# RWKV-7 scan and hard-swish FFN on one core: the decay input w of units 8 to 23 is loaded in 32-token quadrants and turned on VectorE

## The chip, the cores and the metric

The kernel runs on one core of a Trainium2 chip. The metric is device time in microseconds for one execution of the program. The core's engines, as the profile names them: PE (TensorE, matrix products and its weight loads PEld), DVE (VectorE), ACT (ScalarE), POOL (GpSimd) and SP (SyncE, which here issues DMA transfers). Each engine, and SP's queue of transfers too, works through its own instructions in program order.

## The reference

Two blocks follow one another. The first is a recurrence over 768 tokens for each of 4 x 8 heads with a 40 x 40 state; the second a feed-forward block over the 3072 tokens of 320 features.

```python
for t in range(S):                              # r, k, v, w, a, b: (4, 8, 768, 40)
    y[:, :, t] = np.einsum('bhd,bhde->bhe', rt, state)
    Sa = np.einsum('bhde,bhe->bhd', state, at)
    state_decay = state * wt[:, :, None, :] - np.einsum('bhd,bhe->bhde', Sa, bt)
    state = state_decay + np.einsum('bhd,bhe->bhde', vt, kt)
x = attn_out.transpose(0, 2, 1, 3).reshape(B * S, H * D)
h = x @ w_in                                    # (320, 2048)
g = h * np.clip(h + 3.0, 0.0, 6.0) / 6.0
return g @ w_out                                # (2048, 320)
```

What matters here is w: the per-token, per-feature decay. The kernel needs its running products along the tokens.

## The kernel before

**Units.** The recurrence is done in chunks of 64 tokens (`BL`). A unit is one chunk of two batches and all 8 heads; `NU` = 4 units belong to a group and there are `NK` = 24 units, 0 to 23. A unit's input tile has 128 partitions (two batches of 64 tokens) and 8 heads of 64 slots (`SLOT`), of which 40 hold features; the rest is padding, 1.0 for w. Each unit has a part that does not depend on the state (`prepare`, lines 524 to 700) and a part that does (`step`, lines 820 to 1009).

**What the preparation does.** `w_stage` (L527) turns w on TensorE, so that features lie on partitions and tokens along the row: four transposes of 128x128 against an identity (L474, in `turn_pairs`) into a PSUM bank. Two ScalarE copies (L537 and L541) bring it from PSUM into `wm`, the scan's input: 16 rows of 33 per partition, for 4 head pairs, 2 batches and 2 halves of 32 tokens, the first half in reversed token order. Then the next unit's w is fetched, and a VectorE scan (L544) makes the running products. `gam_stage` adds a reciprocal, a second scan (L555) and copies. `a_stage`, `b_stage` and `k_stage` turn a, b and k on TensorE and multiply them with what came out of the scans; `F`, `factor`, `E` and `EV` follow. `factor_stage` multiplies K and B on POOL (L663), then fetches this unit's V (L455) and the next unit's B and K (L458). V is read by the next block's EV products (L690).

**What the step does.** `s_RT` and `s_VT` turn r and v; R, C, U, UT, rS, sn, H and y are products; the result is summed on VectorE (L983, into ys), scaled on POOL (L984, into yg), and `s_move` and `s_move2` put it by eight SBUF-to-SBUF transfers (L998, L1003) into `xt`, the input of the feed-forward block.

**Feed-forward.** `expand` (L1054) makes the hidden products from xt, 96 matrix products to a unit; ScalarE and VectorE apply the activation (L1069, L1070); `contract` (L1095) makes the output, which ScalarE copies (L1113) and SP stores (L1119). It runs as a stream in small pieces between the pieces of the recurrence.

**Order.** The order on every engine is fixed by hand. From group 2 on (units 8 and up) the program goes in blocks, four to a unit's step. In `a_block` a unit in preparation contributes its stages block by block (`AHEAD_STAGES`, or `CLOSE_STAGES` where units follow after three blocks), beside the steps of an earlier unit (`OWN_STAGES`). `together` (L1328) runs the stages of one block: first the TensorE products of all stages, in the order of `PRODUCTS`, as far as five PSUM banks go; then what drains them, in the order of `RESULTS`. `TURNS` are the stages at the head of `PRODUCTS` that take a bank or half a pair each. A stage that is not in `PRODUCTS` is run with the last drain of its block. Transfers are issued by the stages as they come, nearly all on SP's queue. Where an inversion runs (once per group, `invert`), VectorE has many small instructions beside these (L741, L747).

**Loads.** `fetch` (L434) loads one input of one unit: for W, A, B and K one transfer for each of two batches, 64 tokens x 8 heads in rows of 40 floats (160 bytes); for R and V two per batch. W, A, B, K and R of the next unit are fetched when this unit's tile has been read (`following`).

Of the kernel before, what the change touches and what calls it, by code (L numbers as in the profile page):

```python
# [18 lines left out]
BL = 64  # L19
HB = BL // 2  # L20
L = 32
SLOT = 64
# [3 lines left out]
def _ap(ap, extra, dims):  # L26

    return bass.AP(tensor=ap.tensor, offset=ap.offset + extra, ap=[list(ap.ap[0])] + dims)
# [3 lines left out]
def kernel(  # L32
# [42 lines left out]
    nc = tc.nc  # L75
    B, H, T, D = r.shape
# [3 lines left out]
    NU = 2 * NP  # L80
# [38 lines left out]
    def ps_any(shape):  # L119
        tag, bufs = ring[0]  # L120
        ring.rotate(-1)
        at = 0
        if tag == "whole":
            t = pair()
            open_half[0] = None
        elif tag != "pair":
            t = bank(tag, [P, 512], bufs)
        elif open_half[0] is None:
            t = open_half[0] = pair()
        else:  # L130
            t, at = open_half[0], 512
            open_half[0] = None
        views, step = [], 1
        for d in reversed(shape[1:]):
            views.insert(0, [step, d])
            step *= d
        return _ap(t[:], at, views)
# [3 lines left out]
    def ps_pair(*dims):  # L141
# [21 lines left out]
        out=ident[:], in_=ones, pattern=[[1, P]],  # L163
# [4 lines left out]
        out=ones[:, 0:BL], in_=ones[:, 0:BL], pattern=[[1, BL]],  # L168
# [3 lines left out]
        out=ones[BL:P, 0:BL], in_=ones[BL:P, BL:P], pattern=[[1, BL]],  # L172
# [15 lines left out]
    PADS = {"W": 1.0}  # L188
# [18 lines left out]
    SCAN = NB * 2 * (HB + 1)  # L207
# [3 lines left out]
    wms = [const.tile([P, SCAN + 1], F32, name=f"wm{i}") for i in range(2)]  # L211
# [10 lines left out]
    for i in range(3):  # L222
        t = const.tile([P, H, BL], F32, name=f"score{i}")
# [14 lines left out]
    for p in range(NP):  # L238
        t = const.tile([P, 2, NPR, SLOT], F32, name=f"state{p}")
        nc.vector.memset(t[:], 0.0)  # L240
        state.append(t)
        t = const.tile([P, 2, NPR], F32, name=f"last{p}")
# [16 lines left out]
    for i, (x, y) in enumerate([(0, DFF // 2), (0, NJ // 2)]):  # L259
        for n, z in enumerate((x, y)):  # L260
            t = win[:, :, z:z + H * SLOT] if i == 0 else \
                wout[:, z:z + 4, :].rearrange("p j m -> p (j m)")[:, 0:2 * H * SLOT].rearrange(
                    "p (n x) -> p n x", n=2)
            t = t.rearrange("p n (h e) -> p n h e", e=SLOT)
            name = ("WA", "BK")[i][n]
# [3 lines left out]
    for u in range(2):  # L269
        t = win2[:, u * NPR * P:(u + 1) * NPR * P]  # L270
# [160 lines left out]
    names = [(2 * (i // NU) + i % NU // NP, i % NP) for i in range(NK)]  # L431
    data = [{} for _ in range(NK)]

    def fetch(name, i, engine=None):  # L434

        if i is None or i >= NK:
            return
        x, crossed = {"W": (w, 0), "A": (a, 0), "B": (b, 0), "K": (k, 0), "R": (r, 1),
                      "V": (v, 1)}[name]
        if name == "V":  # L440
            t = values[i % AHEAD]
        else:
            t = placed.get((name, i))
            if (name, i) == ("R", 1):
                t = others["K"]
            t = t if t is not None else (others if i < 2 * NU and i % 2 and name != "R" else inputs)[name]
        g, p = names[i]
        engines = engine or nc.sync
        for q in range(2):
            engine = engines[q] if isinstance(engines, tuple) else engines  # L450
            y = x[2 * p + q, :, g * BL:(g + 1) * BL, :]
            rows = slice(q * BL, (q + 1) * BL)
            if crossed:
                for s in range(2):
                    engine.dma_start(out=t[rows, 4 * s:4 * s + 4, 0:D],  # L455
                                     in_=y[s::2].rearrange("h t e -> t h e"))
            else:
                engine.dma_start(out=t[rows, :, 0:D], in_=y.rearrange("h t e -> t h e"))  # L458
        data[i][name + "N"] = t

    def following(i):

        if i < 2:
            return None
        if i < 2 * NU:

            return i + 2 if i % NU < NU - 2 or i % 2 == 0 else None
        return i + 1

    def turn_pairs(x):  # L470

        o = ps_any([P, NPR, P])
        for n in range(NPR):
            nc.tensor.transpose(out=o[:, n, :],  # L474
                                in_=x[:, 2 * n:2 * n + 2, :].rearrange("p s e -> p (s e)"),
                                identity=ident[:])
        return o
# [46 lines left out]
    def prepare(i, F):  # L524
        n, o = i % NU, data[i]
        halves = i >= 2 * NU
        def w_stage():  # L527
            wt = turn_pairs(o["WN"])
            yield PE

            wm = o["wm"] = wms[i % 2]
            wv = wm[:, 0:SCAN].rearrange("p (r m i) -> p r m i", m=2, i=HB + 1)
            x = wt[:].rearrange("p r (q m i) -> p (r q) m i", q=2, m=2)
            if i == 0:
                nc.vector.tensor_copy(wv[:, :, 0, 1:HB + 1], x[:, :, 0, ::-1])
            else:
                nc.scalar.activation(out=wv[:, :, 0, 1:HB + 1], in_=x[:, :, 0, ::-1], func=AF.Copy)  # L537
            if i == 0:
                nc.vector.tensor_copy(wv[:, :, 1, 1:HB + 1], x[:, :, 1, :])
            else:  # L540
                nc.scalar.activation(out=wv[:, :, 1, 1:HB + 1], in_=x[:, :, 1, :], func=AF.Copy)  # L541
            fetch("W", following(i))
            prods = o["prods"] = tmp.tile([P, NB, 2, HB + 1], F32, name="prods", bufs=2)
            nc.vector.tensor_tensor_scan(  # L544
                out=prods[:].rearrange("p r m i -> p (r m i)"), data0=wm[:, 0:SCAN], data1=start[:],
                initial=0.0, op0=ALU.mult, op1=ALU.add,
            )

        def gam_stage():
# [28 lines left out]
            if NU <= i <= 2 * NU:  # L578
                fetch("V", i)
            yield from ()  # L580

        def a_stage():
            x = turn_in(o["AN"], halves)
            yield PE
            nc.vector.memset(_ap(o["wm"][:], 0, [[HB + 1, 2 * NB + 1]]), 0.0)
            at = o["at"] = grp.tile([P, NPR, P], F32, name="at", tag="at")
            for y, z, g in zip(parts_of(at, halves), x, parts_of(o["G"], halves)):
                nc.vector.tensor_tensor(out=y, in0=z, in1=g, op=ALU.mult)
            fetch("A", following(i))
# [93 lines left out]
        def ev_stage():  # L683
# [10 lines left out]
            for x in range(2):  # L694
                nc.scalar.activation(out=EV[half(x)], in_=ev[2][half(x)][:, ::-1] if x else ev[2][half(x)],  # L695
                                     func=AF.Copy)
            o["EV"] = EV

        return {"W": w_stage, "gam": gam_stage, "A": a_stage, "B": b_stage, "F": f_by_32 if i < 2 * NU else f_by_64,
                "factor": factor_stage, "K": k_stage, "E": e_stage, "EV": ev_stage}  # L700

# [524 lines left out]
    n, cleared = 0, []  # L1226
    while not third:
        aside(1)
        if not third:
# [3 lines left out]
            if converted[0] >= 2 and not cleared:  # L1233
                cleared.append(True)
                for z in range(0, P, BL):
                    nc.scalar.activation(out=tinv[z + L:z + BL, :, 0:L], func=AF.Copy, scale=0.0,
                                         in_=_ap(three[z + L:z + BL], 0, [[0, NH], [0, L]]))
# [67 lines left out]
    for _ in range(18):  # L1305
# [10 lines left out]
    CLOSE_STAGES = [["W", "gam"], ["A", "B"], ["F", "K", "factor"], ["E"], ["EV"]]  # L1316


    PRODUCTS = ["W", "S", "K", "RT", "VT", "A", "B", "factor",
                "y", "EV", "R", "C", "U", "UT", "rS", "sn", "H", "E", "F"]  # L1320
    RESULTS = ["RT", "y", "W", "VT", "EV", "R", "S", "C", "A", "B", "move", "move2",
               "U", "UT", "rS", "F", "K", "sn", "H", "E", "factor", "gam"]
    TURNS = PRODUCTS[:3]
    WIDTH = {"R": NPR * D, "U": NPR * D, "sn": NPR * D, "EV": NPR * D}
    BLOCKS = 4
    FIRST_NARROW = PRODUCTS[len(TURNS)]

    def together(stages):  # L1328
# [3 lines left out]
        def finish():  # L1332
            begun.sort(key=lambda x: RESULTS.index(x[0]))
            for _, rest in begun:
                for _ in rest:
                    pass
            begun.clear()
            shared[0] = open_half[0] = None
            ring.clear()
            ring.extend(TURNS_IN)  # L1340

        for name in PRODUCTS:
            if name == FIRST_NARROW and narrow and spread[0] and stages:
                narrow[0]()
            for stage in stages.get(name, []):
                if name in TURNS:
                    need = 2 * (open_half[0] is None) if ring[0][0] == "pair" else 1
# [3 lines left out]
                if banks + need > 5:  # L1351
                    finish()
                    banks, need = 0, 1 if name in TURNS else 2
                banks += need
                rest = stage()
                next(rest)
                begun.append((name, rest))
        begun.extend((name, stage()) for name in stages if name not in PRODUCTS
                     for stage in stages[name])
# [35 lines left out]
    m = 0  # L1395
# [61 lines left out]
```

## Time and profile before

| what | value |
|---|---|
| three runs | 797.92, 798.93, 802.25 us; median 798.93 us |
| span of the profiled execution | 802.0 us |
| granted TensorE clock over the span | 0.956 of full |
| instructions | 35325 |
| SP's DMA issues between 205 and 605 us | 363 |
| DMA packets | 174215, of them 157424 under 512 bytes; 45.03 MB |
| DMA queue of SP (q1) | 169760 packets, 27.7% of the 16 DMA engines' span |
| w transposes on TensorE into the small bank (L474) | 76 in the profile, 273 ns median each |
| ScalarE copies of w (L537, L541) | 24 each, 0.39 us |
| first and second scan (L544, L555) | 24 each, 1.27 and 1.57 us |
| 32x32 turns of the inversion on VectorE, 128x1024 (L721, L750, L755) | 6 each, 2.15, 1.97 and 2.05 us |

Times are from one profiled execution. An engine's busy time is the union of its instructions; issuing a transfer does not count as busy. PE's ends are modelled, so consecutive products overlap in it, and the distance of two starts tells more than one duration. A window is a stretch of the span with the busy time of each engine in it. The timeline merges neighbouring instructions of one line into one row: start, length, engine, line, operation, destination and source, count.

### The profile page before, as it was taken

How to read it: one execution, taken by the hardware profiler on the slowest of the kernel's cores; microseconds unless marked ns; L12 is line 12 of the kernel's file. 1: busy time of each engine (PE TensorE's matmuls, PEld its weight loads, DVE VectorE, ACT ScalarE, POOL GpSimd, SP SyncE). 2: the span in 40 equal slices, each digit the busy share in tenths (PEclk: the TensorE clock that was granted, in tenths of full speed). 3: DMA queues.
4: the chain of work that ended last, by engine and by line, in shares of the span. 5: the costliest groups of instructions: out<-in, count | busy, mean ns of one | idle time of the engine just before them, and what ended most of it. 6: DMA issues, size and time to landing. Idle time of an engine off the chain costs nothing.

```text
span 802.0 us, 35325 instructions
## 1 busy us (share of the span) xinstructions
PE 733.3 (91%) x15832; PEld 622.8 (78%) x15832; DVE 495.5 (62%) x967; ACT 321.2 (40%) x668; POOL 175.6 (22%) x318
## 2 busy tenths in 40 slices
PE   5726777999999989999999999999999999999998
PEld 4625665878778868888888888888888888888886
DVE  7896777679555699455698445897444973322210
ACT  2348882321644424543344453324443324422111
POOL 6403012420322222223123123304122202000000
PEclk9855798999999999999999999999999999999999
DMA  9683553420233331233222233213222101110000
GB/s 120 118 198 85 152 142 57 76 46 9 45 57 66 59 56 28 53 64 56 41 45 43 44 58 62 46 34 57 44 51 48 20 20 29 30 25 13 15 19 17
DMA packets 174215, 45.03 MB, mean 56 GB/s; under 512 B 157424, under 2 KB 172784, under 8 KB 174064
## 3 DMA queue, kind: packets, MB, share of 16 engines
q1 hardware_dynamic: 169760, 42.03, 27.7%
q8 instruction: 125, 2.05, 1.1%
q10 hardware_dynamic: 4304, 0.74, 0.7%
q14 instruction: 26, 0.21, 0.1%
HBM read 34.08 MB, written 3.93 MB: 47 GB/s over the span
## 4 chain that ended last, share of the span: by engine, by line
PE 77%; DVE 8%; issue 5%; DMA 4%; SPq 2%; ACT 2%; POOL 1%; DVEq 0%; ACTq 0%; POOLq 0%
PE h L1054 26%; PE o L1095 24%; PE pair L512 4%; PE pair L972 3%; PE pair L484 2%; PE pair L949 2%; PE one L474 2%; PE pair L894 2%; PE pair L856 2%; PE pair L914 1%; PE pair L690 1%; PE pair L930 1%; DMA R<-in_r_dram 1%; DVE wm L555 1%; PE pair L799 1%
## 5 line engine op out<-in xcount | busy, mean ns | idle before, releaser
L1054 PE MATMUL h<-xt,win 128*128 128x128 f32 (+1 forms) x2304 | 250.4, 282 | 3.5 <-DVE gt L1070 3.5
L1054 PEld LDWEIGHTS h<-xt,win 128*128 128x128 f32 (+1 forms) x2304 | 230.8, 192 | 20.5 <-issue 4.2
L1095 PE MATMUL o<-wout,gt 128*128 128x320 f32 x768 | 231.8, 445 | 0.0
L1095 PEld LDWEIGHTS o<-wout,gt 128*128 128x128 f32 x768 | 139.2, 191 | 51.0 <-issue 1.2
L1070 DVE SCALAR_TENSOR_TENSOR gt<-gt,h 128x512 f32<-128x512 f32 x96 | 62.0, 681 | 71.7 <-ACT gt L1069 71.6
L1069 ACT ACTIVATE gt<-h,three 128x512 f32<-128x512 f32 x96 | 62.2, 686 | 100.9 <-PE h L1054 100.5
L984 POOL TENSOR_TENSOR yg<-ys,gam 128x512 f32<-128x512 f32 x22 | 39.0, 1772 | 165.4 <-DVE ys L983 91.2
L741 DVE TENSOR_TENSOR prod<-x 128x30 f32<-128x30 f32 (+9 forms) x180 | 67.2, 373 | 8.8 <-POOL x L726 3.3
L663 POOL TENSOR_TENSOR KBt<-K,rgt 128x320 f32<-128x320 f32 x22 | 19.0, 865 | 215.4 <-ACT rgt L652 166.9
L747 DVE TENSOR_TENSOR x<-x,prod 128x30 f32<-128x30 f32 (+9 forms) x180 | 62.3, 346 | 5.5
L957 DVE TENSOR_TENSOR state<-pair,state 40x320 f32<-40x320 f32 (+1 forms) x44 | 21.4, 487 | 65.9 <-PE pair L949 39.8
L520 DVE COPY_PREDICATED score<-mask,pair 128x512 f32<-128x512 int32 x71 | 49.9, 723 | 1.8 <-PE pair L512 1.4
L983 DVE TENSOR_TENSOR ys<-pair,ys 128x512 f32<-128x512 f32 x22 | 15.2, 691 | 44.7 <-PE pair L690 22.0
L555 DVE TENSOR_TENSOR_SCAN wm<-wm,start 128x528 f32<-128x528 f32 x24 | 37.6, 1565 | 0.8
L544 DVE TENSOR_TENSOR_SCAN prods<-wm,start 128x528 f32<-128x528 f32 x24 | 30.3, 1270 | 10.2 <-ACT wm L541 10.1
L834 ACT ACTIVATE RT<-pair 128x512 f32<-128x512 f32 x21 | 12.5, 597 | 52.9 <-PE pair L484 52.9
L972 PE MATMUL pair<-score,KBt 64*64 64x64 f32 x1472 | 29.2, 232 | 4.0 <-DVE state L957 3.2
L695 ACT ACTIVATE EV<-pair 64x320 f32<-64x320 f32 x44 | 19.0, 432 | 33.5 <-PE pair L690 22.8
L972 PEld LDWEIGHTS pair<-score,KBt 64*64 64x64 f32 x1472 | 25.8, 145 | 6.6 <-DVE state L957 3.7
L809 ACT ACTIVATE tinv<-pair 32x256 f32<-32x256 f32 x48 | 18.0, 375 | 30.1 <-PE pair L799 29.5
L1113 ACT ACTIVATE ob<-o 128x320 f32<-128x320 f32 x22 | 9.6, 435 | 49.1 <-PE o L1095 29.3
L572 POOL COPY gam<-prods 128x256 f32<-128x256 f32 x24 | 22.5, 937 | 29.3 <-DVE prods L544 25.4
(262 smaller groups left out, 1062.6 us busy)
## 6 DMA issues: line engine op xcount, KB each, us to landing
V<-in_v_dram SPq DMA_DIRECT2D x96, 40.0 KB
out_dram<-ob SPq DMA_DIRECT2D x47, 80.0 KB
R<-in_r_dram SPq DMA_DIRECT2D x92, 40.0 KB
B<-in_b_dram SPq DMA_DIRECT2D x42, 80.0 KB
K<-in_k_dram SPq DMA_DIRECT2D x42, 80.0 KB
W<-in_w_dram SPq DMA_DIRECT2D x37, 80.0 KB
A<-in_a_dram SPq DMA_DIRECT2D x37, 80.0 KB
xt<-yg SPq DMA_DIRECT2D x72, 40.0 KB
```

What stands on the lines that cost most here:

```text
L512: nc.tensor.matmul(out=o[i][half(q), n, :], lhsT=lhs[half(i, D), n ^ (2 * q * swap), half(q)], rhs=rhs[half(i, D), n, half(q)], start=True ...
L520: nc.vector.copy_predicated(out=x[:].rearrange("p (i h) t -> p i h t", i=2), mask=mask8, data=o[2])
L544: nc.vector.tensor_tensor_scan(out=prods[:].rearrange("p r m i -> p (r m i)"), data0=wm[:, 0:SCAN], data1=start[:], initial=0.0, op0=ALU.m ...
L555: nc.vector.tensor_tensor_scan(out=back, data0=back, data1=start[:], initial=0.0, op0=ALU.mult, op1=ALU.add)
L741: nc.vector.tensor_tensor(out=pv, in0=_ap(x[:], (i + 1) * L + i, [[L, n], [0, i]]), in1=_ap(x[:], i * L, [[0, n], [1, i]]), op=ALU.mult,)
L747: nc.vector.tensor_tensor(out=rest, in0=rest, in1=pv, op=ALU.add)
L972: nc.tensor.matmul(out=y[q][half(s), pr, :], lhsT=o[name][half(q), h * D:h * D + SLOT], rhs=m[name][half(q), 4 * rs + 2 * s + j, :], start ...
L984: nc.gpsimd.tensor_tensor(out=yg[:], in0=m["ys"][:].rearrange("p r q t -> p r (q t)"), in1=o["G"][:], op=ALU.mult)
L1054: nc.tensor.matmul(out=hp[c][:, i, :], lhsT=lhsT, rhs=rhs, start=(begun[c] == 0), stop=(begun[c] == 3 * NQ - 1))
L1069: nc.scalar.activation(out=gt[:], in_=hp[c][:], func=AF.Relu, bias=three[:], scale=1.0)
L1070: nc.vector.scalar_tensor_tensor(out=gt[:], in0=gt[:], scalar=6.0, in1=hp[c][:], op0=ALU.min, op1=ALU.mult)
L1095: nc.tensor.matmul(out=op[:], lhsT=gts[c][:, n, :], rhs=wout[:, c * HJ + r * NQ + n, :], start=((split or r == 0) and c == 0 and n == 0), ...
```

## The change

For units 8 to 23, w is no longer loaded as whole 64-token rows and turned by TensorE. A new helper, `fetch_blocks`, loads it in pieces of 32 tokens: for two heads of a pair (s), two parts of the features (0 to 31 and 32 to 39, n), two batches (q) and two token halves (m), 16 transfers in all, each of 32 partitions x 4 heads with rows of 32 or 8 floats. In the tile the 32 partitions are tokens of a quadrant and every 32 slots along the row hold one 32x32 square. Two VectorE transposes turn all squares in place of partition and row, straight into `wm`, the first half with its tokens reversed. The padding squares are set to 1.0 once, at unit 8, by two POOL memsets. The tile, the scan and everything after it are the same. In the planner's lists W leaves `PRODUCTS` (and so `TURNS`) and comes first in `RESULTS`.

```diff
+        if name == "W" and i >= 2 * NU:
+            fetch_blocks(t, w, i)
+            data[i]["WN"] = t
+            return
...
+    PARTS = [(0, L), (L, D - L)]
+
+    def fetch_blocks(t, x, i):
+
+        g, p = names[i]
+        to = by_blocks(t)
+        if i == 2 * NU:
+            for s in range(2):
+                z = s * SLOT + L
+                nc.gpsimd.memset(t[z:z + L, :, :], PADS["W"])
+        for s in range(2):
+            for n, (at, width) in enumerate(PARTS):
+                rows = slice(s * SLOT + n * L, s * SLOT + n * L + L)
+                for q in range(2):
+                    y = x[2 * p + q, s::2, g * BL:(g + 1) * BL, at:at + width]
+                    for m in range(2):
+                        nc.sync.dma_start(out=to[rows, q::2, m, 0:width],
+                                          in_=y[:, m * HB:(m + 1) * HB].rearrange("h t e -> t h e"))
+
+    def by_blocks(t):
+        return t[:].rearrange("p h e -> p (h e)").rearrange("p (n m e) -> p n m e", m=2, e=L)
...
         def w_stage():
+            if halves:
+                x = by_blocks(o["WN"])
+                wv = scanned()
+                nc.vector.transpose(out=wv[:, :, 0, HB:0:-1], in_=x[:, :, 0, :])
+                nc.vector.transpose(out=wv[:, :, 1, 1:HB + 1], in_=x[:, :, 1, :])
+                decays()
+                return
             wt = turn_pairs(o["WN"])
...
+            decays()
+
+        def scanned():
+            wm = o["wm"] = wms[i % 2]
+            return wm[:, 0:SCAN].rearrange("p (r m i) -> p r m i", m=2, i=HB + 1)
+
+        def decays():
+            wm = o["wm"]
             fetch("W", following(i))
...
-    PRODUCTS = ["W", "S", "K", "RT", "VT", "A", "B", "factor",
+    PRODUCTS = ["S", "K", "RT", "VT", "A", "B", "factor",
                 "y", "EV", "R", "C", "U", "UT", "rS", "sn", "H", "E", "F"]
-    RESULTS = ["RT", "y", "W", "VT", "EV", "R", "S", "C", "A", "B", "move", "move2",
+    RESULTS = ["W", "RT", "y", "VT", "EV", "R", "S", "C", "A", "B", "move", "move2",
                "U", "UT", "rS", "F", "K", "sn", "H", "E", "factor", "gam"]
-    TURNS = PRODUCTS[:3]
+    TURNS = PRODUCTS[:2]
```

More of the change, by code (lines that the diff above doesn't have):

```diff
@@ L527, in w_stage @@
         def w_stage():
+            if halves:
[5 more added lines that the diff above has]
+                return
             wt = turn_pairs(o["WN"])
             yield PE
-            wm = o["wm"] = wms[i % 2]
-            wv = wm[:, 0:SCAN].rearrange("p (r m i) -> p r m i", m=2, i=HB + 1)
+            wv = scanned()
             x = wt[:].rearrange("p r (q m i) -> p (r q) m i", q=2, m=2)
```

## The prediction

> **What bounds the kernel now.** I read the page first, then TensorE in windows, the SP queue's timeline, and the chain of waits where it leaves TensorE. The page's first part says that TensorE is the bound:
>
> ```profile
> PE 733.3 (91%) x15832; PEld 622.8 (78%) x15832; DVE 495.5 (62%) x967; ACT 321.2 (40%) x668; POOL 175.6 (22%) x318
> ```
>
> In the windows from 205 us on it is almost never idle (second column the stretch, then busy time of PE, PEld, DVE, ACT, POOL):
>
> ```profile
> 205.00:310.00 105.00, 99.22 (x2413) 83.05 (x2415) 68.41 (x143) 44.37 (x106) 25.18 (x46) 1.00 0.30 53
> 400.00:510.00 110.00, 109.55 (x2577) 93.79 (x2574) 72.40 (x139) 47.82 (x107) 27.79 (x43) 1.00 0.26 49
> ```
>
> So less TensorE work should shorten the end, if TensorE goes on being fed. Its feeding passes through one queue: nearly every load and every xt move is issued by SP, in program order. One unit of it, in the timeline (start, length, line, issues):
>
> ```profile
> 455.29 2.75 SPq L455 DMA_DIRECT2D V<-in_v_dram  x4
> 459.01 1.27 SPq L458 DMA_DIRECT2D B<-in_b_dram  x2
> 460.33 1.30 SPq L458 DMA_DIRECT2D K<-in_k_dram  x2
> 461.74 2.64 SPq L455 DMA_DIRECT2D R<-in_r_dram  x4
> 464.43 1.69 SPq L458 DMA_DIRECT2D W<-in_w_dram  x2
> 466.52 1.18 SPq L1119 DMA_DIRECT2D out_dram<-ob  x2
> 468.42 1.40 SPq L458 DMA_DIRECT2D A<-in_a_dram  x2
> 469.94 3.12 SPq L998 DMA_DIRECT2D xt<-yg  x4
> 473.41 2.66 SPq L1003 DMA_DIRECT2D xt<-yg  x4
> 480.56 3.52 SPq L455 DMA_DIRECT2D V<-in_v_dram  x4
> ```
>
> The reader is to see two things. An issue takes 0.6 to 0.65 us whatever it moves: four L1003 moves of 32 rows in about 2.5 us, two B loads of 512 rows each in 1.27 us. And the 26 issues of this unit fill 18.0 of the 25.3 us to the next V. What TensorE reads sits in that queue. The chain of waits, which is TensorE nearly everywhere, shows it between 253 and 265 us, where it goes through SP and the landings:
>
> ```profile
> 254.56 1.55 SPq L455
> ...
> 256.15 2.27 DMA V<-in_v_dram
> ...
> 262.21 2.77 DMA K<-in_k_dram
> ```
>
> The slack of those loads is small. TensorE's timeline has the first product of a unit's xt (96 L1054 products to a unit, counted in order) and its first product with V at:
>
> ```profile
> 483.02 1.95 PE L1054 MATMUL h<-xt,win 128*128 128x128 f32 x16
> 487.90 0.63 PE L690 MATMUL pair<-V,score 64*64 64x40 f32 x32
> ```
>
> These are units 12 and 18. The xt moves above end at 476.1 and land some 2 us later: 5 us spare. The V issued from 480.56 lands at 485.8: 2 us spare. Over units 12 to 23 V has 1.0 to 4.9 us, and xt of units 4 to 19 between nothing and 13 us (nine of the sixteen under 4); both are read off SP's and TensorE's timelines and the landings.
>
> **The change part by part.** The profiled execution spans 802.0 us, 3.1 us over the median of the runs (798.93); I sum against 802.0 and apply the difference to the median.
>
> Removed from TensorE: 16 units x 4 transposes.
>
> ```profile
> L474 PE MATMUL one<-ident,W 128*128 128x128 f32 x76 | 12.0, 282 | 4.5 <-DMA W<-in_w_dram 4.5
> ```
>
> The 282 ns overlap; four follow one another at 0.11 us, and the chain gives a set 0.44 us. With TensorE full, 16 x 0.45 = -7.2 us. Removed from ScalarE: 32 copies (L537, L541) x 0.389 = 12.4 us of 321, off the path: nothing. The PSUM bank they used is free sooner: bounded by TensorE's waits for evacuations between 205 and 615 us, about 3 us in all; nothing taken.
>
> Added to VectorE: two 32x32 turns of 128x256. Nearest are L721, L750 and L755, 1.97 to 2.15 us for 128x1024, so a quarter, 0.51 us, twice; 16 x 1.03 = 16.5 us. VectorE is busy 62% and takes it in its idle time: nothing. Without that cover, in the four later inversions, 4 x 1.03 = 4 us. W is now drained first in its group, so turns and first scan (1.03 + 1.25 us) stand ahead of the ys sum (L983); that feeds yg and the xt moves, but yg was ready at 404.4 us and its moves went out at 412.0, so nothing. The sixteen loads now wait for VectorE's turns, not TensorE's; queued behind them on SP are R (16 us spare and more, as it is fetched a unit ahead), the output, A and xt. Two POOL memsets, once: the nearest (L224) is 0.53 us; POOL is 22% busy.
>
> Added to the DMA engines: 2048 rows of 128 or 32 bytes for 1024 of 160. The queue's 169760 packets took 27.7% of 16 x 802 us, 21 ns each; 1024 more are 1.3 us on each engine per unit, at 24 to 30% load: nothing.
>
> Added to SP: a unit's W takes 16 issues, not 2. No row shows this shape. Below is the cheapest common load, L328's at about 0.42 us; above, the mean of all SP issues from 205 to 605 us, 0.71 us, with the long ones in. Nearest are V, R (0.61) and L1003 (0.588), so 0.60; with 0.045 us between issues 16 x 0.645 - 1.3 = **9.0 us per unit** (6.1 to 10.8). Does it fit? SP's issue time plus that, against the stretch:
>
> - 205 to 309 us, five W: 66.5 + 45 = 111.5 against 104.4
> - 309 to 391, three: 54.9 + 27 = 81.9 against 82.1
> - 391 to 455, two: 38.3 + 18 = 56.3 against 63.8
> - 455 to 507, two: 36.2 + 18 = 54.2 against 52.1
> - 507 to 572, two: 34.6 + 18 = 52.6 against 64.6
> - 572 to 598, one: 20.1 + 9 = 29.1 against 26.0
>
> So SP is full, and it can't use the time in which it must wait for its releases (V's buffer is free only after L949, and the xt moves stand behind A's load, which waits for A's transposes). What that does to TensorE I took from a walk along the trace. Each SP issue keeps its length, the W pairs get 9.0 us more; an issue that came after idle time starts no earlier than before plus the delay so far, the others when the one ahead ends; each lands as long after its issue as before. Where V, A, B, K or xt lands after its first TensorE use plus the delay so far, the difference is added. The delay grows by 4.2 us at 160 to 162 (B of units 6 and 7, queued behind the first sixteen), 9.2 at 247 to 290 (B of units 10 to 12), 17.3 at 242 to 336 (xt of units 4, 6, 7), 9.5 at 420 to 454 (xt of 10, 11), 3.5 at 485 to 517 (V of 18, 19, xt of 12) and 8.4 at 536 to 603 (xt of 14 to 16): 52.0 us. Sum: 802.0 - 7.2 + 52.0 = 846.8, and against the median **844**; I take 842, since a rigid walk lets no other slack help. With 8.0 us per unit the walk gives +30 net, with 10.0 +61.
>
> The Trainium skill ("DMA: Bandwidth & Descriptors", section "Issuing engines are not separate DMA queues") says that the sequencer's time to start a DMA is usually small beside the DMA itself. Here it is 0.63 us beside a landing after 2.7 us, but in a queue that is two thirds full. By the rule the added issues would cost nothing; that is the second rival below.
>
> **The rivals.**
> 1. Long issues. A tenth of SP's issues take 0.97 us and more; with 0.71 us for the new ones (10.8 per unit) the walk goes to some +72: **871**. For: those rows. Against: the median is 0.63.
> 2. SP's lateness is hidden and TensorE's saving stays, the other side: 798.9 - 7.2 = **792**. The sign turns where the walk's net is nothing, at 4 us per unit or 0.29 us an issue; or if xt and V could come 9 us later. For: TensorE is at 99%, SP idle a third of the time. Against: the slack of 1 to 9 us.
> 3. Cheap issues: at 0.42 us (+6.1 per unit) the walk gives +11 net, 810. For: L328's loads. Against: V, R and L1003 with 32 to 256 rows all at 0.59 us and over.
> 4. VectorE sets the pace, with W's turns and scan ahead of the ys sum: 16 x 2.3 - 7 = +30, 829, with SP idle. Against: 62% busy, and yg done long before its moves.
> That the change doesn't do what it says I see no way for.
>
> **Numbers.** Forecast 0.63 (own range 826 to 860), rival 1 0.12, rival 2 0.09, rival 3 0.12, rival 4 0.04. The range 808 to 871 takes in all but rival 2 and the far tails. Measured against 0.5% (4 us, what can be told from no change): faster 0.08, same 0.03 (part of rivals 2 and 3), slower 0.89.
>
> **What would show it.** SP's queue with sixteen W issues in a row of about 0.6 us, back to back over most of 205 to 600 us; L1054 and L690 with idle time released by xt and V landings; PE busy near 726 us in a longer span, VectorE near 512, ScalarE near 309. Wrong if TensorE stays at 99% with no wait for a DMA, if the new issues take 0.3 us, or if TensorE's new idle time is released by VectorE while SP has gaps.

## The result, and the profile after

The changed kernel takes 848.43 us (median of 4 runs, 846.26 to 848.94) against 798.42 us (four runs of the kernel before; the table above has three of them): 1.0618 times as long, with a 95% interval from 1.0589 to 1.0646. Its profiled execution spans 846.4 us. From its page, the lines of TensorE, of the chain by engine, and of the hidden products (L1094, which was L1054):

```profile
PE 741.9 (88%) x15768; PEld 628.6 (74%) x15768; DVE 510.7 (60%) x999; ACT 312.4 (37%) x636; POOL 170.3 (20%) x320
...
PE 59%; SPq 8%; DVE 6%; DMA 4%; issue 3%; ACT 2%; POOL 1%; DVEq 0%; ACTq 0%
...
L1094 PE MATMUL h<-xt,win 128*128 128x128 f32 (+1 forms) x2304 | 260.4, 289 | 26.0 <-DMA xt<-yg 20.0
```

The last two of these in the kernel before:

```profile
PE 77%; DVE 8%; issue 5%; DMA 4%; SPq 2%; ACT 2%; POOL 1%; DVEq 0%; ACTq 0%; POOLq 0%
...
L1054 PE MATMUL h<-xt,win 128*128 128x128 f32 (+1 forms) x2304 | 250.4, 282 | 3.5 <-DVE gt L1070 3.5
```

Three things are to be seen. TensorE has 64 instructions fewer and yet is busy longer, 741.9 us against 733.3. SP's queue now holds 8% of the chain that ended last (2% before; the listed shares add up to 83% here and to 99% before, so SPq's rise says more than PE's fall). And the hidden products, which before hardly waited (3.5 us), wait 20.0 us for xt to land. TensorE's idle time is 846.4 - 741.9 = 104.5 us, 35.8 us more than before. The windows that were shown of before, in the changed kernel:

```profile
205.00:310.00 105.00, 90.89 (x2114) 73.78 (x2114) 58.46 (x112) 38.97 (x87) 25.79 (x50) 0.92 0.29 47
400.00:510.00 110.00, 102.11 (x2196) 87.23 (x2196) 75.18 (x148) 39.85 (x86) 24.50 (x43) 0.97 0.26 44
```

TensorE has fallen from 94.5% to 86.6% in the first and from 99.6% to 92.8% in the second, and the granted clock (third number from the end) from 1.00 in both to 0.92 and 0.97. One unit of SP's queue, in its timeline:

```profile
491.55 3.06 SPq L459 DMA_DIRECT2D V<-in_v_dram  x4
495.27 1.27 SPq L462 DMA_DIRECT2D B<-in_b_dram  x2
496.60 1.31 SPq L462 DMA_DIRECT2D K<-in_k_dram  x2
498.01 9.54 SPq L481 DMA_DIRECT2D W<-in_w_dram  x16
507.64 2.74 SPq L459 DMA_DIRECT2D R<-in_r_dram  x4
510.47 1.20 SPq L1159 DMA_DIRECT2D out_dram<-ob  x2
511.77 1.70 SPq L462 DMA_DIRECT2D A<-in_a_dram  x2
513.56 3.12 SPq L1038 DMA_DIRECT2D xt<-yg  x4
516.72 2.96 SPq L1043 DMA_DIRECT2D xt<-yg  x4
519.78 2.75 SPq L459 DMA_DIRECT2D V<-in_v_dram  x4
```

W takes 9.54 us where it took 1.69, the queue has hardly a gap between two V, and the xt moves stand behind the sixteen. What TensorE waits for from 140 us on, in the view of waits (in total, times, longest):

```profile
PE h L1094 <- DMA xt<-yg: 20.0, 6, 7.2
PE pair L510 <- DMA B<-in_b_dram: 6.7, 4, 3.1
PE one L500 <- DMA B<-in_b_dram: 5.3, 1, 5.3
...
PE pair L730 <- DMA V<-in_v_dram: 2.6, 3, 1.3
```

These 34.6 us are loads and moves that SP issued late; the kernel before has no wait for a DMA in that view. The remaining 8.6 us of the 44.4 are TensorE being busy longer; where they come from can be seen around the longest of these waits. The windows before it, in it and behind it:

```profile
348.90:352.30 3.40, 3.40 (x133) 2.63 (x132) 0.69 (x1) 2.04 (x5) 0.00 (x0) 1.00 0.17 21
352.30:359.50 7.20, 0.02 (x1) 0.05 (x1) 0.00 (x0) 1.40 (x5) 0.00 (x0) 0.76 0.30 59
359.50:362.90 3.40, 3.40 (x16) 3.40 (x16) 0.00 (x0) 0.00 (x0) 0.00 (x0) 0.50 0.08 18
362.90:369.70 6.80, 6.80 (x188) 5.94 (x189) 3.58 (x7) 1.70 (x3) 2.05 (x4) 1.00 0.16 27
```

TensorE stands for 7.2 us, and then runs at a granted clock of 0.50 for 3.4 us, in which it gets 16 products done. So this stall costs its own 7.2 us, and then up to half of the 3.4 us that follow.

### The profile page after: what moved, and what is told of

Same layout as the page of the kernel before. It is cut to its first block, busy times and chain, and to the rows that moved or that the text cites. A ratio compares the mean times of both kernels' runs of the same rounds, so it can differ in the third digit from the quotient of the medians.

```text
span 846.4 us, 35497 instructions
## 1 busy us (share of the span) xinstructions
PE 741.9 (88%) x15768; PEld 628.6 (74%) x15768; DVE 510.7 (60%) x999; ACT 312.4 (37%) x636; POOL 170.3 (20%) x320
## 4 chain that ended last, share of the span: by engine, by line
PE 59%; SPq 8%; DVE 6%; DMA 4%; issue 3%; ACT 2%; POOL 1%; DVEq 0%; ACTq 0%
PE h L1094 23%; PE o L1135 18%; SPq L1038 3%; PE pair L538 3%; PE pair L510 2%; SPq L459 2%; PE pair L1012 2%; SPq L1043 2%; PE pair L896 1%; PE pair L989 1%; DMA V<-in_v_dram 1%; PE pair L934 1%; DMA xt<-yg 1%; SPq L462 1%; PE one L500 1%
## 5 line engine op out<-in xcount | busy, mean ns | idle before, releaser
L1094 PE MATMUL h<-xt,win 128*128 128x128 f32 (+1 forms) x2304 | 260.4, 289 | 26.0 <-DMA xt<-yg 20.0
L1094 PEld LDWEIGHTS h<-xt,win 128*128 128x128 f32 (+1 forms) x2304 | 240.5, 198 | 44.2 <-issue 25.1
L1024 POOL TENSOR_TENSOR yg<-ys,gam 128x512 f32<-128x512 f32 x22 | 29.2, 1325 | 177.7 <-DVE ys L1023 100.2
L595 DVE TENSOR_TENSOR_SCAN wm<-wm,start 128x528 f32<-128x528 f32 x24 | 42.8, 1781 | 0.8
L584 DVE TENSOR_TENSOR_SCAN prods<-wm,start 128x528 f32<-128x528 f32 x24 | 30.3, 1269 | 2.5 <-ACT wm L573 1.9
L692 ACT ACTIVATE rgt<-pair 128x320 f32<-128x320 f32 x16 | 7.0, 438 | 60.6 <-DVE state L997 60.6
L900 DVE TENSOR_TENSOR RR<-pair,EV 128x320 f32<-128x320 f32 x21 | 10.3, 489 | 30.0 <-PE pair L538 29.7
```

Source lines behind the costliest of these rows:

```text
L584: nc.vector.tensor_tensor_scan(out=prods[:].rearrange("p r m i -> p (r m i)"), data0=wm[:, 0:SCAN], data1=start[:], initial=0.0, op0=ALU.m ...
L595: nc.vector.tensor_tensor_scan(out=back, data0=back, data1=start[:], initial=0.0, op0=ALU.mult, op1=ALU.add)
L1024: nc.gpsimd.tensor_tensor(out=yg[:], in0=m["ys"][:].rearrange("p r q t -> p r (q t)"), in1=o["G"][:], op=ALU.mult)
L1094: nc.tensor.matmul(out=hp[c][:, i, :], lhsT=lhsT, rhs=rhs, start=(begun[c] == 0), stop=(begun[c] == 3 * NQ - 1))
```

## The experiments

The theory: SP issues its transfers one by one, sixteen pieces per unit make it late, and TensorE waits behind it; the stalls lower the clock besides. Rival A: VectorE's turn and the drain order carry the loss. Rival B: the many small rows load the DMA engines. Rival C: every unit's pieces cost a fixed amount. Ratios are to the kernel before, run beside each experiment on the same chip.

| kernel | median us | before us | ratio, 95% interval |
|---|---|---|---|
| the change | 848.43 | 798.42 | 1.0618 [1.0589, 1.0646] |
| e1 pieces alone | 847.01 | 799.65 | 1.0594 [1.0567, 1.0620] |
| e2 turns alone, 2 pieces | 802.38 | 799.65 | 1.0046 [1.0022, 1.0071] |
| e3 eight pieces | 811.20 | 799.65 | 1.0154 [1.0112, 1.0197] |
| e5 pieces on POOL | 911.95 | 799.65 | 1.1418 [1.1374, 1.1461] |
| e6 two pieces throughout | 798.08 | 799.84 | 0.9977 [0.9956, 0.9998] |
| e7 rows alone | 801.10 | 799.84 | 1.0017 [1.0005, 1.0028] |
| e8 eight, later | 803.30 | 799.84 | 1.0045 [1.0030, 1.0061] |
| e9 eight on ScalarE | 815.47 | 799.84 | 1.0197 [1.0172, 1.0223] |
| e10 old drain order | 799.93 | 799.66 | 0.9997 [0.9980, 1.0014] |
| e11 eight, later, old order | 802.65 | 799.66 | 1.0033 [1.0010, 1.0056] |
| e12 from unit 13 | 797.54 | 799.66 | 0.9975 [0.9958, 0.9992] |
| e13 every second unit | 804.49 | 799.70 | 1.0056 [1.0034, 1.0077] |

**The pieces alone (e1).** The kernel before, with this in `fetch`:

```diff
+            elif name == "W" and i >= 2 * NU:
+                for s in range(2):
+                    for at, width in (0, L), (L, D - L):
+                        for m in range(2):
+                            z = q * BL + m * HB
+                            engine.dma_start(out=t[z:z + HB, s::2, at:at + width],
+                                             in_=y[s::2, m * HB:(m + 1) * HB, at:at + width].rearrange("h t e -> t h e"))
```

> The kernel before, with w of units 8 to 23 loaded in the change's 16 pieces (same rows of 32 and 8 floats, same queue), but into the old layout and turned by TensorE as before; nothing else differs. Theory (SP's queue is late and TensorE waits behind it; the stalls then lower the granted clock): slower by about what the change lost plus the 7 us of TensorE work that is not saved, 845 to 860 us, with TensorE waits released by xt, B and V landings and half-clock stretches after them. Rival A (VectorE's turns and the drain order carry the loss): within 5 us of before. The walk of the prediction with the 7.9 us per unit that the changed kernel's trace shows gives +33 us without the clock.

847.01 us: the loads alone, with TensorE's turn and ScalarE's copies as before, cost 47.4 us, against 50.0 for the whole change. Its waits from 140 us on, and TensorE's line of its page:

```profile
PE h L1061 <- DMA xt<-yg: 18.1, 6, 6.7
PE one L481 <- DMA W<-in_w_dram: 6.0, 1, 6.0
PE pair L491 <- DMA B<-in_b_dram: 4.8, 4, 2.6
PE one L481 <- DMA B<-in_b_dram: 4.6, 1, 4.6
```
```profile
PE 747.4 (88%) x15832; PEld 634.5 (75%) x15832; DVE 495.6 (59%) x967; ACT 321.3 (38%) x668; POOL 176.6 (21%) x318
```

The same kinds of waits as in the change, and one for W itself, which TensorE still turns here. The work on TensorE is that of before, and it is busy 14.1 us longer (747.4 against 733.3) and idle 30.8 us longer (99.5 against 68.7); together the 44.9 us by which this execution is longer. The walk of the prediction, given 7.9 us per unit, has 33 us for the idle part. Rival A is out as the cause of the loss.

The change saves the TensorE work that e1 still does, and yet it is not faster than e1. TensorE is busy 5.5 us less in it and idle 5.0 us more. From 140 us on its waits for DMA come to the same in both (34.6 and 34.9 us), while those for VectorE are 7.8 us in the change and 3.9 in e1. What that is, e6 and e10 show.

**The turn alone (e2).** The change, with 14 of the 16 pieces left out for units 9 and up:

```diff
                     for m in range(2):
+                        if i > 2 * NU and (n or s):
+                            continue
+                        if i > 2 * NU and m:
+                            continue
```

> The changed kernel, but for units 9 to 23 only 2 of the 16 pieces of w are loaded (one per batch, first features, first token half); the rest of the tile keeps what unit 8 left in it, so the output is not the reference's. TensorE, ScalarE, VectorE and the order are those of the change; SP has as many issues as before. Theory (SP's queue): faster than before by the 7 us of TensorE transposes, 790 to 796 us, less some us for unit 8's sixteen pieces, so up to 800. Rival A (VectorE's turns, or the drain order): slower than before, 815 us or more.

802.38 us: 46 us of the 50 are gone, so A is out again as their cause, but it is over the 790 to 800 that were expected. In its trace TensorE stands for 5.1 us at 157 us, where B of unit 6 is late behind unit 8's sixteen pieces, and has the half clock for 6.8 us from 159 us on. e6 takes these pieces away.

**Eight pieces (e3).** The batches in one transfer, the tile's blocks batch by batch:

```diff
-                for q in range(2):
-                    y = x[2 * p + q, s::2, g * BL:(g + 1) * BL, at:at + width]
-                    for m in range(2):
-                        nc.sync.dma_start(out=to[rows, q::2, m, 0:width],
+                y = x[2 * p:2 * p + 2].rearrange("q h t e -> (q h) t e")[s::2, g * BL:(g + 1) * BL, at:at + width]
+                for m in range(2):
+                    nc.sync.dma_start(out=to[rows, :, m, 0:width],
```

> The changed kernel with both batches of a piece in one transfer (the tile's blocks stand batch by batch, and the turn reads them in that order): 8 issues per unit instead of 16, the same rows and bytes. Theory (the number of SP issues): 8 x 0.575 - 1.3 = 3.3 us per unit, for which the walk gives -2 us net, so 793 to 805 us and hardly a half-clock stretch. Rival B (the many small rows load the DMA engines): as slow as the change, 835 us or more. Rival A: 815 us or more.

811.20 us with the same rows and bytes: 37 us less than the change, so the number of issues decides and not the rows, but the 793 to 805 were missed. The walk itself was not far off: its -2 us net are 5.2 us of waits less the 7.2 us saved, and from 140 us on TensorE waits 7.0 us for DMA. What it leaves out is 8.9 us of waits for VectorE (3.7 in the kernel before), and half-clock stretches from 208 and 457 us, in which TensorE is busy for 10.2 us (3.4 before). That W's issues now stand ahead of R was not tried by itself.

**The pieces on POOL's queue (e5).** `nc.gpsimd.dma_start` for `nc.sync.dma_start` in `fetch_blocks`.

> The changed kernel with the 16 pieces issued by POOL's queue, not SP's. Theory (SP's queue): TensorE waits for xt and V go; 790 to 800 us if POOL has room for 16 issues in its 80% idle time, more (800 to 830) if an issue holds POOL so long that yg or KBt come late, which would then show as waits for POOL. Rival B (small rows load the DMA engines): 835 us or more. Rival A: 815 us or more with waits for VectorE.

911.95 us, far over the range. Its waits of TensorE:

```profile
PE one L918 <- DVE state L883: 40.8, 9, 8.9
PE h L1094 <- DVE gt L1110: 31.3, 4, 10.2
```

No wait for xt or V, as the theory has it; but POOL waits before its sixteen issues until VectorE has turned the tile, and then issues for 16 x 0.55 us, and behind it in its order are the scale of the state and the other copies that VectorE needs: VectorE waits 103.8 us for that scale, against 6.2 us before. The experiment moved the blockade to a queue whose work is nearer to the path. It says nothing against or for rival B.

**Two pieces throughout (e6).** As e2, with `if n or s or m: continue` for all units.

> As e2, but unit 8 too gets only 2 of its 16 pieces (the rest of the tile keeps what unit 6 left), so SP issues exactly as many transfers as before everywhere; the output is not the reference's. Theory: e2's loss against its forecast came from unit 8's sixteen pieces ahead of B of units 6 and 7 (a TensorE gap of 5.1 us at 157 us and a half-clock stretch of 6.8 us after it); without them 791 to 796 us. Rival A (the turn on VectorE, ahead of the ys sum, eats the TensorE saving): 799 us or more, as e2.

798.08 us: 4.3 us less than e2, so unit 8's sixteen pieces did cost that. But the turn, free of any extra issue, gains 1.8 us (0.2 to 3.5 by the interval), not 7. TensorE's waits from 140 us on begin with

```profile
PE h L1096 <- DVE gt L1112: 3.4, 3, 1.7
PE one L920 <- DVE state L885: 1.9, 1, 1.9
```

against 0.6 us of the first and none of the second in the kernel before. The first are three waits of the hidden products for VectorE's part of the activation, at 283, 403 and 519 us. Each falls within an inversion, between its first and its last 128x1024 turn on VectorE (273 to 315, 382 to 430 and 499 to 546 us). From 280 to 300 us, for one, VectorE was busy 19.0 of 20 us before, and now it has the turn to do too. The second, for the state, is at 204 us, just behind an inversion, with the turn and the first scan ahead of it on VectorE. In all, TensorE waits 8.3 us for VectorE from 140 us on, against 3.7 before.

**The rows alone (e7).** The kernel before, with w in two parts of the features, 4 issues and 2048 rows per unit:

```diff
+            elif name == "W" and i >= 2 * NU:
+                for at, width in (0, L), (L, D - L):
+                    engine.dma_start(out=t[rows, :, at:at + width],
+                                     in_=y[:, :, at:at + width].rearrange("h t e -> t h e"))
```

> The kernel before, with w of units 8 to 23 loaded in the change's 2048 rows per unit (32 and 8 floats), but in 4 issues of 512 rows instead of 16; old layout, turned by TensorE as before. Theory (number of issues): two more issues, 1.2 us per unit, within 3 us of before, 798 to 803 us. Rival B (small rows): 830 us or more. In between (the descriptors are counted too): 805 to 825.

801.10 us, 1.3 us over before, as the theory had it. Rival B is out: the rows of 32 and 8 floats cost nothing like the loss.

**Eight pieces, later (e8).** e3, with W fetched in the K stage (units 13 and up) and, for unit 8, in the EV stage of unit 6:

```diff
-            fetch("W", following(i))
+            if i != 2 * NU - 2 and i < 3 * NU:
+                fetch("W", following(i))
...
             nc.vector.tensor_tensor(out=kt[:], in0=x[:], in1=o["rg"][:], op=ALU.mult)
+            if i >= 3 * NU:
+                fetch("W", following(i))
...
             o["EV"] = EV
+            if i == 2 * NU - 2:
+                fetch("W", following(i))
```

> e3 (8 issues per unit) with the loads put elsewhere in SP's order: for units 13 and up behind the xt moves (issued in the K stage instead of the W stage), for unit 8 behind B, K and V of units 6 and 7 (in the EV stage of unit 6); units 9 to 12 as in e3. Theory (what stands behind the pieces in SP's queue decides): xt no longer waits for them, so e3's 811 falls to 793 to 803 us, the shift against before now only between units 5 and 7. If only the number of issues counted: 808 to 812 as e3.

803.30 us, just over what was expected: 7.9 us less than e3 with the same issues. TensorE's waits for DMA from 140 us on fall from 7.0 to 1.6 us. What stands behind the pieces in the queue decides as well as their number.

**Eight pieces on ScalarE's queue (e9).** e8 with `nc.scalar.dma_start` in `fetch_blocks`.

> e8 with the eight pieces issued by ScalarE's queue instead of SP's. Theory: SP has two issues fewer than before, so no TensorE wait for xt or V; ScalarE is busy 39% and gets 8 x 0.58 = 4.6 us per unit in a place where the turns are long done (units 13 and up), 792 to 805 us. If a ScalarE that issues transfers holds up the activations in its order: 805 to 825 us with TensorE waits released by ACT.

815.47 us, slower than e8, with these waits from 140 us on:

```profile
PE pair L509 <- ACT VT L913: 6.2, 2, 3.8
...
PE pair L509 <- ACT UT L966: 4.8, 1, 4.8
```

ScalarE, 38% busy, has no room for the issues where they fall: its copies of VT and UT come late. The shift against before comes between 197 and 304 us (the first hidden products of units 3 and 6), where W of units 9 to 12 is still fetched right behind the turn; later it grows no more.

**The old drain order (e10), and with it the whole computation (e11).** `RESULTS` begins with RT and y again, W behind them, in e6 and in e8.

> e6 (2 pieces throughout, the rest of w left out) with W back behind RT and y in the drain order, as in the kernel before; W is still no TensorE product. Theory: e6 gained only 2 of 7 us because turn and first scan (0.40 + 0.44 + 1.26 us) now stand on VectorE ahead of the state scaling and the ys sum that TensorE waits for (1.9 us for the state at 204 us); with the old order 792 to 796 us. If the order costs nothing and the missing 5 us lie elsewhere (in how runs vary, or in the turn itself): 797 to 799 us as e6.

> e8 (8 issues, placed behind the xt moves) with the old drain order; the whole computation. Theory: e8's 803.3 less what e10 gains against e6, 797 to 801 us. If the drain order costs nothing: 803 us.

799.93 and 802.65 us: both as without it (798.08 and 803.30), within what the runs vary. That theory falls: the drain order costs nothing that can be measured. In e10 the wait for the state at 204 us is gone, but one of 1.8 us for another VectorE result (wm, at 205 us) stands in its place, and the three waits for gt are there as before. TensorE's waits for VectorE from 140 us on are 8.4 us, 8.3 in e6, 3.7 in the kernel before. So most of the 5 to 7 us of TensorE's saving that are missing go to waits for VectorE, which does the turn in and behind its inversions whatever the drain order. This is read from the waits; no run moved the turn out of the inversions.

**From unit 13 (e12).** e11, with the turn for units 13 and up alone (`TURNED = 3 * NU + 1`) and before's `PRODUCTS`, `RESULTS` and `TURNS`.

> e11 for units 13 to 23 alone; units 8 to 12, whose blocks follow one another after three blocks and fill SP's queue, load and turn w as the kernel before, and the planner's lists are those of before. The whole computation. Theory: 11 x 0.45 = 5 us of TensorE saved and none of the B waits of the dense stretch: 794 to 797 us, faster than both kernels. If the turn's saving isn't realised at all: 799 to 801 us.

797.54 us, 0.25% faster than before (0.08% to 0.42%), and some 51 us faster than the change. It beats both, by less than was expected: the forecast was 794 to 797. The 2.1 us are also less than the 4 us that the prediction took as the least that can be told from no change, though the interval leaves out 1. Its waits for VectorE from 140 us on are 5.7 us, between the two kernels.

**Every second unit (e13).** e1 with `and i % 2` in its condition: 8 units in pieces, 112 added issues in place of 224.

> e1 (the kernel before with w in 16 pieces), but only for the odd units 9 to 23, 8 units instead of 16. Theory (a queue that is late only where it cannot catch up before the next sixteen): the walk with 7.9 us per piece-loaded unit gives +2 us for the odd units against +33 for all, so 800 to 806 us and no half-clock stretch after 200 us. Rival C (each unit's pieces cost what they cost, one by one, by stalls or otherwise): half of e1's 47 us, 818 to 828 us.

804.49 us: 4.8 us over before, not 24. Its wait for xt from 140 us on is one:

```profile
PE h L1061 <- DMA xt<-yg: 1.3, 1, 1.3
```

With those for B, TensorE's waits for DMA are 3.0 us. Half of the pieces cost a tenth of the loss, in part because unit 8's sixteen, which cost some 4 us by e2 and e6, are not among them. Rival C is out all the same, as half of the remaining 43 us would still be some 21: SP catches up in the unit between, and it is the lateness carried from unit to unit that reaches TensorE.

## Why the prediction held, by its own steps

It forecast 842 us and 848.4 were measured, for the reason it gave; but its sum, 846.8 against the profile's 846.4, is as near as that by luck: two errors of 16 us cancel.

- **SP per unit, 9.0 us: mis-sized.** Sixteen issues took 9.2 us on average, 7.9 more than the 1.3 that the prediction put for the two before (on average those took 1.6). A piece takes 0.53 us on average and 0.43 in the median; 0.60 was taken from loads of 256 and 512 rows and from moves of 32 rows. A piece has 128 rows, and the reading that an issue takes the same whatever it moves was too coarse.
- **The walk, 52.0 us: right in kind, too large by that error.** With 7.9 us it gives about 36 us of added waits (its own points are 52 at 9.0 and 37 at 8.0); TensorE's idle time grew by 35.8. In e1 it gives 33 against 30.8, in e3 5.2 against 7.0 us of waits for DMA, in e13 2 against 4.8 us of the whole time. The parts fit less well than the sum. For B it had 13.4 us and 12.0 were measured. For xt it had 27 us on units 4, 6, 7, 10 and 11, and more on 12 and 14 to 16; of the 20.0 us measured, 18.8 fall on units 7, 11 and 15, and no wait for xt of units 4, 6, 10, 12 or 14 reaches 0.4 us.
- **The clock: left out.** TensorE was expected to be busy 726 us and was 741.9, 15.8 us more. From 140 us on it is busy for 33.7 us inside half-clock stretches of the trace's clock record, against 3.4 us in the kernel before; at half the clock the 30.3 us more are some 15 us of added time, an estimate that accounts for nearly all of it. Not every stretch is SP's doing: the one of 6.8 us from 213 us on follows a wait for VectorE. These 15.8 us and the 16 us too many in the walk are the two errors.
- **TensorE's saving, -7.2 us: hardly realised.** In e6, with SP as before, 1.8 us are left of it, in e10 none that can be measured. The step that failed here is the turn on VectorE at nothing. Its cover by idle time (62% busy) is an average; the prediction named the inversions as the place where it is gone, at 4 us, and left them out of the sum. TensorE's waits for VectorE from 140 us on grew by 4.6 us in e6, 4.7 in e10 and 4.1 in the change.
- **The turn, 2 x 0.51 us:** it took 0.43 and 0.40 us.

```profile
L557 DVE STREAM_TRANSPOSE wm<-W 128x256 f32<-128x256 f32 x16 | 6.9, 432 | 0.0
L558 DVE STREAM_TRANSPOSE wm<-W 128x256 f32<-128x256 f32 x16 | 6.5, 404 | 0.0
```

- **Small rows, drain order, POOL's memsets at nothing:** right by e7 and e10; the memsets took 0.52 us each.
- **The rivals.** Long issues: a part of the new issues do take 0.6 to 1.9 us, but the mean is 0.53. Hidden lateness: no, as the slack of xt and V had said. Cheap issues: half right, the median is 0.43, yet with the long ones in a unit's sixteen still take 9.2 us. VectorE as the bound: no, by e1 and e2; it costs some 4 us and not 30.

## What to carry to other kernels

A load split into pieces is paid for on the queue that issues it: count the issues of one period, multiply by the measured time of one, and compare with the period, before asking what the bytes cost. An engine that is over 99% busy can still be slowed through the queue that feeds it, if that queue is two thirds full and the inputs land 1 to 5 us ahead of their use. Work that moves to a second engine is not free in the stretches where that engine is full, whatever its average. Ask what stands behind the new issues in their queue, and whether the queue can catch up before they come again: the same pieces cost 47 us in every unit and 5 us in every second.

## What the runs showed of the hardware

- **A stall can be paid for twice.** After TensorE's gap of 7.2 us at 352 us the granted clock was 0.50 until 362.9 us: 16 hidden products ran at a mean of 423 ns, against 288 ns in the next 6.8 us. The trace's clock record has seven such stretches of 3.4 or 6.8 us after 140 us in the changed kernel, each during or right after one of its gaps of 1.9 to 7.2 us, and the kernel before has one of 3.4 us ahead of the tail, from 176 us on, behind a gap of 1.6 us at 172.5 us. In e6, e7 and e12, whose longest gap after 140 us is 1.9 us, there is none but in the tail. The Trainium skill ("TensorE: Matmul & The Clock Gate", section "Part 1: The HAM clock gate") says that a free-running window of about 3.4 us of idle halves the clock; the lengths of these stretches agree. Here gaps shorter than that, 1.9 us at 210 us in the changed kernel, also had a half-clock stretch behind them, while the one of 1.9 us at 204 us in e6 had none.
- **An issue on SP's queue holds it 0.4 to 0.8 us in the median, with a tail to 2.0 us.** A piece of 128 rows took 0.43 us, one of e3's of 256 rows 0.45, e7's loads of 512 rows 0.63. The rows alone don't set it: V's loads of 256 rows took 0.62 us and the second xt moves, of 32 rows, 0.59. What does was not tried.
- **An idle engine isn't a free queue.** POOL at 20% and ScalarE at 37% busy in the changed kernel took the issues worse than SP (911.95 against 848.43 us for sixteen, 815.47 against 803.30 for eight): in e5 POOL stood 23.8 us before its issues, each held it 0.55 us, and what stands behind them in its order came late.
